# Attention, Fourier mixing and feed-forward: scores made once, probabilities and normalized rows turned by transfers

## The chip, the cores and the metric

The kernel runs on one core of a Trainium2 chip. The metric is the device time of one execution in microseconds (us). TensorE (PE) multiplies matrices into PSUM, eight banks of 128 partitions by 2 KB; VectorE (DVE), ScalarE (ACT) and GpSimd (POOL) work on tiles of up to 128 partitions in SBUF; transfers run on 16 DMA engines and are issued from the queues of SyncE (SP), ACT and POOL. Each queue takes its instructions in order, so an instruction that waits holds up what stands behind it.

## The reference

Inputs are q, k and v of 8 batches, 8 heads, 576 positions, 64 values a head, and two weight matrices of 512 x 2048 and 2048 x 512, all float32.

1. Attention by heads, with a mask by blocks of 64 positions: position i sees j where `i // 64 >= j // 64`. Scores are scaled by 1/8, the maximum of a row is subtracted, then come the exponential, the division by the row's sum (plus 1e-9) and the product with v.
2. The heads are put side by side: x has 8 x 576 x 512.
3. `u = x + real(fft(fft(x, axis=1), axis=2))`.
4. `un = (u - mean) / sqrt(var + 1e-6)` along the 512 values.
5. `out = u + max(un @ w_ch1, 0) @ w_ch2`.

## The kernel before

**Precision.** float32 operands are cut in two parts that are multiplied apart: a rounded part and a rest, or a high and a low half in f16. So a score is `LEAD x LEAD` plus one matmul of 128 rows in which `REST` holds rest and rounded part stacked, and an f16 product is three matmuls (high x high, high x low, low x high).

**A head.** `load_head` (line 288) brings q and k, turned on the host, to `raw` (64 x 1152). `lead` rounds it on ACT into one of three `LEAD` buffers, two transfers copy its halves into `REST` (`lead_copies`), and DVE and POOL write the rests (`rest`). Rows 64 to 71 of `LEAD` hold constants that put the mask into the product. Then comes a first pass for the maxima, `max_part`: matmuls of `LEAD` alone, with queries on the partitions, six of them with 1600 columns in all, and reductions on DVE into `M`. `shift` turns `M` (128 x 5) by a matmul with the identity, scales it on ACT and sends it by a transfer into row 72 of `LEAD`. In the second pass `scores` makes the scores again, now in both parts and with keys on the partitions, since the values need keys there; row 72 subtracts the maximum within the product. ACT takes the exponential twice, to f16 (`ph`) and to float32, and POOL subtracts them (`pl`). `values` multiplies with v in 15 pairs of blocks, three matmuls each, into one bank `av`; DVE divides by the sum, and for each second head two transfers store the pair to a buffer `xd` in DRAM.

**A batch.** When its eight heads are stored, `mirror` loads the rows and, by POOL's indirect transfers, their mirror images; sums and differences go through cosine and sine matrices (`stage1`, `stage2_sin`, `stage2_cos`). `normalized_steps` takes two row tiles of 128 at a time, normalizes them (`norm`), and `turn` turns each with four matmuls with the identity into a bank, from which ACT takes the high half `uh` and DVE the low half `ul`. There are 18 such pairs, 36 tiles. Each pair gives a stretch of feed-forward work (`feed_steps`): 192 matmuls of 256 columns (into bank `h`) and 96 of 512 (into bank `acc`).

**Weights.** In the front 18 loads of the weights (14 of 1 MB, 4 of 512 KB) are issued from SP, three in flight, and DVE, ACT and POOL cut them in two parts.

**Order.** A planner in the kernel writes the order of PE's instructions. Each `Step` has a cost on PE, a chain of what follows on other engines (`D`, `A`, `G`, `Q` for DVE, ACT, POOL and SP's queue with a time, `L` for a transfer's landing, `B` for the point where its bank is free) and the steps that it must follow. Lanes (loads, preparing, maxima, scores, values, transforms) hand over their next step; the planner takes the one that is ready by its own clock, and fills with feed-forward matmuls when none is. On the chip PE takes matmuls in this order, whatever the other engines are late by. Before all weights have landed no second batch's heads are begun. Banks: three named `ps`, two `h`, two `acc`; from the first feed-forward step on only `ps` serve attention and transforms.

Of the kernel before, what the change touches and what calls it, by code (L numbers as in the profile page):

```python
# [44 lines left out]
KM = D + 8  # L45
KS = KM + 1

# [24 lines left out]
def _constants():  # L72
# [45 lines left out]
    masks = np.zeros((9, 64 + 2 * S))  # L118
    masks[8, 64 + S:] = 1.0
    for c in range(4):  # L120
        masks[c, 64 + 128 * c:128 + 128 * c] = 1.0
        masks[c, 64 + S + 128 * c + 64:64 + S + 128 * c + 128] = NEG
        masks[4 + c, 128 + 128 * c:192 + 128 * c] = 1.0
        masks[4 + c, 64 + S + 128 * c + 128:64 + S + 128 * c + 192] = NEG
# [6 lines left out]
        "c_id": np.eye(P, dtype=np.float32),  # L131
# [5 lines left out]
class Step:  # L137
# [8 lines left out]
    bank: bool = False  # L146
# [32 lines left out]
def tile_attn_fourier_ffn(  # L179
    ctx: ExitStack, tc: tile.TileContext, qk, v, w1, w2, c_dft, c_masks, c_id, c_rows, out  # L180
# [9 lines left out]
    def ps_tile():  # L190
        return ps[current].tile([P, 512], F32, name=current)
# [4 lines left out]
    def tp(*args, **kw):  # L196
        return tc.keep_in_program_order(nc.tensor.transpose(*args, **kw))  # L197


    ident = const.tile([P, P], F32, name="ident")  # L200
    nc.sync.dma_start(ident, c_id)
# [21 lines left out]
    NB = 3  # L223
    LEAD = [const.tile([KS, 64 + 2 * S], F32R, name=f"lead{i}") for i in range(NB)]
    REST = [const.tile([P, 2 * S], F32R, name=f"rest{i}") for i in range(NB)]
    M = [const.tile([P, 6], F32, name=f"M_{i}") for i in range(2)]
# [4 lines left out]
    for i in range(NB):  # L231
        nc.gpsimd.dma_start(LEAD[i][D:KS], c_masks)
        nc.vector.tensor_scalar(LEAD[i][0:D, 0:64], ones[0:D, 0:64], 0.0, None, op0=ALU.mult)
    for i in range(2):
        nc.vector.memset(VH[i][:, 0:4, :, D:D + 1], 1.0)
        nc.vector.memset(VH[i][0:64, 4, :, D:D + 1], 0.0)
        nc.vector.memset(VH[i][64:128, 4, :, D:D + 1], 1.0)
# [12 lines left out]
    current = "ps"  # L250
# [5 lines left out]

    def ready(step):
        r = max((done[x] for x in step.after), default=0.0)
        return max(r, min(rings[x][0] for x in lent)) if step.bank else r

    def issue(step):
# [15 lines left out]
        if step.bank:  # L277
            current = min(lent, key=lambda x: rings[x][0])
            rings[current] = rings[current][1:] + [t if free is None else free]
# [15 lines left out]
    def quick(h):  # L295

        return nc.scalar if h < H else nc.sync

    def lead_copies(h):
        x0, x1 = REST[h % NB].bitcast(F32), LEAD[h % NB].bitcast(F32)  # L300
        quick(h).dma_start(x0[D:P, 0:S], x1[0:D, 64:64 + S])
        quick(h).dma_start(x0[0:D, S:], x1[0:D, 64 + S:])

    def rest(h, which):

        x0, x1, raw = REST[h % NB], LEAD[h % NB].bitcast(F32), raws[h]
        if which == 0:
            nc.vector.tensor_tensor(x0[0:D, 0:S], raw[:, 0:S], x1[0:D, 64:64 + S], op=ALU.subtract)  # L308
        else:
            nc.gpsimd.tensor_tensor(x0[D:P, S:], raw[:, S:], x1[0:D, 64 + S:], op=ALU.subtract)  # L310
# [38 lines left out]
    def prepare_lane():  # L349
        for h in range(B * H):  # L350
            yield Step(
                lambda: lead(h), 0.0, ("A1.15",), (("L", h),), ("T", h), place=h - 1.0,
                need=(("S", h - NB, 2),) if h >= NB else (),
            )
            yield Step(lambda: lead_copies(h), 0.0, ("A1.0" if h < H else "Q1.2", "L2.2"), (("T", h),), ("TC", h), place=h - 0.9)
# [3 lines left out]
    def v_lane():  # L359
        for g in range(B * H // 2):  # L360
# [4 lines left out]
                       need=(("V", 2 * g - 3, 4),) if g > 1 else ())  # L365
            yield Step(
                lambda: split_v(g), 0.11, ("D0.46", "B", "A0.83", "D0.88"), (("NS", g),), ("N", g), True,
                need=(("V", 2 * g - 3, 4),) if g > 1 else (), place=2 * g - 0.4,
            )

    def max_part(h, n):

        m = M[h % 2]
        x = LEAD[h % NB][0:KM]
        kh = x[:, 64 + S:]
        qh = lambda j: x[:, P * j:P * (j + 1)]
        t = ps_tile()

        parts = MAXPARTS[n]
        at = 0  # L380
        for i, (j, lo, hi) in enumerate(parts):
            mm(
                t[:, at:at + hi - lo], qh(j), kh[:, lo:hi], start=(i == 0), stop=(i == len(parts) - 1),
                skip_group_check=True,
            )
            at += hi - lo
        if n == 0:
            nc.vector.tensor_reduce(
                m[:, 0:6:5], t[:, 0:128].rearrange("p (x y) -> p x y", y=64), axis=AX.X, op=ALU.max
            )  # L390
        j, lo, hi = parts[-1]
        nc.vector.tensor_reduce(m[:, j:j + 1], t[:, at - hi:at], axis=AX.X, op=ALU.max)  # L392
        if n == 3:
            nc.vector.tensor_tensor(m[:, 4:5], m[:, 4:5], m[:, 5:6], op=ALU.max)

    MAXPARTS = (((0, 0, 64), (4, 512, 576), (1, 0, 192)), ((2, 0, 320),), ((3, 0, 448),), ((4, 0, 512),))

    def shift(h):

        t = ps_tile()  # L400
        tp(t[0:5, 0:P], M[h % 2][:, 0:5], ident)
        mt = work.tile([5, P], F32R, name="mt", bufs=2)
        nc.scalar.activation(mt, t[0:5, 0:P], AF.Copy, bias=float(8.0 * PSHIFT * np.log(2.0)), scale=-1.0)
        dst = LEAD[h % NB][KM:KS, 0:640].rearrange("r (j p) -> r j p", j=5)
        quick(h).dma_start(dst.bitcast(F32), mt.bitcast(F32))

    probs = {}

    CHUNKS = (0, 1, 4, 2, 3)
    PIECES = (
        (0, 0, ((0, 0, 288),)), (0, 288, ((0, 288, 288),)),
        (1, 0, ((1, 0, 448), (4, 0, 64))), (2, 0, ((2, 0, 320), (3, 0, 192))),
    )

    def scores(h, n):

        x0, x1 = REST[h % NB], LEAD[h % NB]
        i, at, chunks = PIECES[n]  # L420
        if at == 0:
            width = S if i == 0 else 512
            probs[h, i] = [work.tile([P, width], F16, name=f"p{x}{i}", bufs=1) for x in "hl"]
        ph, pl = probs[h, i]
        t = ps_tile()
        w = 0
        for c, lo, width in chunks:
            first, last = P * c + lo, P * c + lo + width
            keys = S + (P * c if c < 4 else S - P)
            mm(t[:, w:w + width], x0[:, keys:keys + P], x0[:, first:last], start=(w == 0), stop=False, skip_group_check=True)  # L430
            keys, w = keys + 64, w + width
            mm(t[:, w - width:w], x1[:, keys:keys + P], x1[:, 64 + first:64 + last], start=False, stop=True, skip_group_check=True)
        p32 = work.tile([P, 512], F32, name="p32", bufs=2)
        nc.scalar.activation(ph[:, at:at + w], t[:, 0:w], AF.Exp, scale=0.125)  # L434
        nc.scalar.activation(p32[:, 0:w], t[:, 0:w], AF.Exp, scale=0.125)  # L435
        nc.gpsimd.tensor_tensor(pl[:, at:at + w], p32[:, 0:w], ph[:, at:at + w], op=ALU.subtract)  # L436
# [4 lines left out]
    def values(h, at):  # L441
# [6 lines left out]
        c = CHUNKS[at]  # L448
# [12 lines left out]
        if at < 4:  # L461
            return
# [215 lines left out]
    def normalized_steps(us, keys, stores, place):  # L678
# [17 lines left out]
        def turn(i):  # L696
            un = uns.pop(i)
            if i == 0:
                parts.extend(work.tile([P, NK, 2, P], F16, name=x, bufs=2) for x in ("uh", "ul"))
# [313 lines left out]
```

## Time and profile before

Times and profile are of the program on the chip; a share of busy time is of the span.

| | us |
|---|---|
| median of three runs | 1312.41 (1312.14 to 1313.05) |
| profiled execution | 1315.5 |
| its span | 1313.7 |
| PE busy | 1184.2 (90%) |
| DVE busy | 671.9 (51%) |
| ACT busy | 548.5 (42%) |
| POOL busy | 530.0 (40%) |
| DMA: moved bytes | 99.10 MB, 75 GB/s on average |

In the rows of the profile, L194 is the helper that issues every matmul and L197 the one that issues every turn on PE, so matmuls are told apart by their tiles: `ps<-lead 72*128` is the first pass, `73*128` with `rest` the second, `ident,M` the turn of the maxima, `ident,un` that of normalized rows. SPq stands for SP's queue. A group shows its busy time in us, the mean of one in ns, then the idle time of the engine ahead of it and what ended that. The start of a row in a timeline is counted from the start of the span.

### The profile page before, as it was taken

The page shows a single profiled execution, that of the slowest core. Times are in us where ns is not written, and L with a number is a line of the kernel's source. Part 1 is how long each engine was busy: PE and PEld are TensorE (multiplying, and loading weights), DVE is VectorE, ACT ScalarE, POOL GpSimd, SP SyncE. Part 2 cuts the span into 40 slices and gives each one's busy share as a digit, 9 for nine tenths or more (in the row PEclk, how much of TensorE's full clock was granted, in tenths as well). Part 3 has the DMA queues.
Part 4 walks back from the last instruction along what each step waited for, and adds up shares of the span by engine and source line. Part 5 has one row for each costly group of instructions (what it writes and reads, how often), then busy time and mean ns, then how long its engine had stood idle before and what let it go on. Part 6 is the DMA issues. An engine that isn't in the chain of part 4 may idle for free.

```text
span 1313.7 us, 25264 instructions
## 1 busy us (share of the span) xinstructions
PE 1184.2 (90%) x10068; PEld 886.7 (67%) x10068; DVE 671.9 (51%) x1440; ACT 548.5 (42%) x1137; POOL 530.0 (40%) x578
## 2 busy tenths in 40 slices
PE   3464469999898999999999999999899999999998
PEld 2363357777676777677777777777677767767665
DVE  6983776445645564655546544746372432412211
ACT  3569355545354444444545354544543112111110
POOL 4668143444544553455443645436442500300000
PEclk9955679999699999999999999999999999999999
DMA  9756213232223223322242133223211000000000
GB/s 280 230 175 177 93 29 77 84 106 64 61 65 92 76 50 90 93 76 51 80 115 75 44 96 104 73 70 86 79 30 49 30 12 17 22 1 17 16 17 17
DMA packets 55941, 99.10 MB, mean 75 GB/s; under 512 B 7709, under 2 KB 26605, under 8 KB 55696
## 3 DMA queue, kind: packets, MB, share of 16 engines
q1 hardware_dynamic: 52176, 87.56, 23.5%
q0 software_dynamic: 2288, 7.54, 1.9%
q10 hardware_dynamic: 1360, 2.38, 0.6%
q8 instruction: 80, 1.31, 0.4%
q14 instruction: 37, 0.30, 0.1%
HBM read 58.46 MB, written 18.87 MB: 59 GB/s over the span
## 4 chain that ended last, share of the span: by engine, by line
PE 76%; DVE 10%; ACT 4%; DMA 3%; POOL 3%; issue 3%; SPq 0%; ACTq 0%; DVEq 0%; POOLq 0%
PE h L194 27%; PE acc L194 26%; PE ps L194 16%; PE av L194 5%; POOL pl L436 2%; PE ps L197 1%; DVE M L392 1%; DVE W L837 1%; DMA W<-in_moe_w_ch_dram 1%; DVE rest L308 1%; DVE W L838 1%; ACT lead L293 1%; DVE tmp L549 1%; DMA U<-xd,rows 1%; DVE W L836 1%
## 5 line engine op out<-in xcount | busy, mean ns | idle before, releaser
L194 PE MATMUL h<-uh,W 128*128 128x256 f16 x2304 | 434.9, 275 | 0.0
L436 POOL TENSOR_TENSOR pl<-p,ph 128x288 f16<-128x288 f32 (+1 forms) x256 | 257.9, 1017 | 395.8 <-ACT p L435 249.6
L194 PEld LDWEIGHTS <-W 128*128 128x128 f16 x3456 | 325.8, 99 | 64.3 <-issue 4.0
L194 PE MATMUL acc<-W,gh 128*128 128x512 f16 x1152 | 347.2, 383 | 0.0
L194 PE MATMUL h<-ul,W 128*128 128x256 f16 x1152 | 316.2, 274 | 0.0
L194 PE MATMUL acc<-W,gl 128*128 128x512 f16 x576 | 220.1, 382 | 0.4 <-DVE gl L750 0.4
L750 DVE SCALAR_TENSOR_TENSOR gl<-h,gh 128x512 f16<-128x512 f32 x144 | 98.9, 687 | 227.3 <-ACT gh L749 227.2
L194 PE MATMUL ps<-lead 72*128 72x64 f32 (+9 forms) x700 | 196.5, 342 | 12.5 <-ACT lead L293 6.8
L749 ACT ACTIVATE gh<-h 128x512 f16<-128x512 f32 x144 | 85.9, 596 | 268.4 <-PE h L194 267.7
L434 ACT ACTIVATE ph<-ps 128x512 f16<-128x512 f32 (+1 forms) x229 | 116.0, 507 | 121.0 <-PE ps L194 119.7
L194 PEld LDWEIGHTS <-gh 128*128 128x128 f16 x1152 | 101.0, 99 | 87.8 <-issue 8.2
L392 DVE TENSOR_REDUCE M<-ps 128x1 f32<-128x320 f32 (+3 forms) x235 | 120.5, 527 | 47.9 <-PE ps L194 46.7
L194 PE MATMUL av<-VH,pl 128*128 128x65 f16 x960 | 115.9, 200 | 31.7 <-POOL pl L436 31.5
L194 PEld LDWEIGHTS ps<-lead 72*128 72x128 f32 (+1 forms) x700 | 125.6, 201 | 20.8 <-ACT lead L293 6.8
L194 PEld LDWEIGHTS <-ph 128*128 128x128 f16 x1920 | 113.0, 103 | 34.1 <-DVE x L474 8.4
L310 POOL TENSOR_TENSOR rest<-raw,lead 64x576 fp32r<-64x576 f32 x64 | 116.2, 1816 | 23.3 <-ACT lead L293 18.5
L194 PE MATMUL av<-VH,ph 128*128 128x65 f16 x960 | 118.1, 202 | 8.2 <-DVE x L474 7.6
L194 PE MATMUL ps<-rest 128*128 128x64 f32 (+2 forms) x345 | 121.6, 360 | 1.8 <-DVE M L392 1.1
L435 ACT ACTIVATE p<-ps 128x512 f32<-128x512 f32 (+1 forms) x229 | 115.9, 506 | 10.2 <-POOL pl L436 10.1
L194 PE MATMUL av<-VL,ph 128*128 128x64 f16 x960 | 117.3, 200 | 0.0
L194 PEld LDWEIGHTS <-pl 128*128 128x128 f16 x960 | 93.6, 102 | 34.9 <-POOL pl L436 34.8
L308 DVE TENSOR_TENSOR rest<-raw,lead 64x576 fp32r<-64x576 f32 x64 | 60.0, 938 | 88.4 <-ACT lead L293 88.3
(171 smaller groups left out, 1376.7 us busy)
## 6 DMA issues: line engine op xcount, KB each, us to landing
raw<-in_qk_dram SPq DMA_DIRECT2D x64, 288.0 KB
rest<-lead SPq DMA_DIRECT2D x112, 144.0 KB
W<-in_moe_w_ch_dram SPq DMA_DIRECT2D x14, 1024.0 KB
V<-in_v_dram SPq DMA_DIRECT2D x32, 320.0 KB
xd<-x SPq DMA_DIRECT2D x32, 256.0 KB
out_dram<-u SPq DMA_DIRECT2D x32, 256.0 KB
u<-xd SPq DMA_DIRECT2D x8, 512.0 KB
dft<-in_c_dft_dram POOLq DMA_DIRECT2D x1, 2606.0 KB, 11.3
```

Of the source, the lines that this page charges most:

```text
L194: return tc.keep_in_program_order(nc.tensor.matmul(*args, **kw))
L197: return tc.keep_in_program_order(nc.tensor.transpose(*args, **kw))
L293: nc.scalar.copy(LEAD[h % NB][0:D, 64:], raws[h])
L308: nc.vector.tensor_tensor(x0[0:D, 0:S], raw[:, 0:S], x1[0:D, 64:64 + S], op=ALU.subtract)
L310: nc.gpsimd.tensor_tensor(x0[D:P, S:], raw[:, S:], x1[0:D, 64 + S:], op=ALU.subtract)
L392: nc.vector.tensor_reduce(m[:, j:j + 1], t[:, at - hi:at], axis=AX.X, op=ALU.max)
L434: nc.scalar.activation(ph[:, at:at + w], t[:, 0:w], AF.Exp, scale=0.125)
L435: nc.scalar.activation(p32[:, 0:w], t[:, 0:w], AF.Exp, scale=0.125)
L436: nc.gpsimd.tensor_tensor(pl[:, at:at + w], p32[:, 0:w], ph[:, at:at + w], op=ALU.subtract)
L549: nc.vector.tensor_tensor(e[0:r], X[c][0:r], U[c][0:r], op=op)
L749: nc.scalar.activation(gh, t, AF.Relu)
L750: nc.vector.scalar_tensor_tensor(gl, t, 0.0, gh, op0=ALU.max, op1=ALU.subtract)
```

## The change

The scores are made once, in both parts, with queries on the partitions. The maxima are taken from them; the exponential takes `-max/8 + 5 ln 2` as a bias, one value a partition. High and low half of the probabilities are written, query by query, into a tile `PROB` (two sets of three tiles: query blocks 4, 0 and 1 in 1024 columns, block 3 in 512, block 2 in 384). One transfer per tile, issued from SP's queue, turns both halves, piece of 128 x 128 by piece, into `TURN` (one set), and `values` reads `TURN`. The key blocks are shifted by 64 rows so that the half block stands first; columns that the mask hides are set to zero once. The first pass, the turn of the maxima and its transfer are gone; `LEAD` has 68 rows, and there are two `LEAD` and `REST` in place of three. The copies of the first eight heads go from ACT's queue to SP's, the weight loads from SP's to ACT's. Of the normalized rows, ACT and DVE now make both halves before the turn, and one transfer from SP's queue turns the two; the identity matrix is gone. The space for POOL's DMA descriptors goes from 8192 to 2048.

```diff
-KM = D + 8
-KS = KM + 1
+KM = D + 4
+SCORES = (
+    (((4, 0, 288), (1, 0, 192)), ((4, 288, 576), (0, 0, 64))),
+    (((3, 0, 448),),),
+    (((2, 0, 320),),),
+)
+WIDTHS = (1024, 512, 384)
+BLOCKS = (((4, 0), (0, 640), (1, 768)), ((3, 0),), ((2, 0),))
...
-    NB = 3
+    NB = 2
+    PROB = [[const.tile([P, 2, w], F16, name=f"prob{i}_{x}") for i, w in enumerate(WIDTHS)] for x in range(2)]
+    TURN = [const.tile([P, 2 * w // P, P], F16, name=f"turn{i}") for i, w in enumerate(WIDTHS)]
...
     def lead_copies(h):
-        quick(h).dma_start(x0[D:P, 0:S], x1[0:D, 64:64 + S])
-        quick(h).dma_start(x0[0:D, S:], x1[0:D, 64 + S:])
+        nc.sync.dma_start(x0[D:P, 64:64 + S], x1[0:D, 64:64 + S])
+        nc.sync.dma_start(x0[0:D, 64 + S:], x1[0:D, 64 + S:])
...
-    def max_part(h, n):
...
-    def shift(h):
...
     def scores(h, n):
         x0, x1 = REST[h % NB], LEAD[h % NB]
+        prob = PROB[h % 2][n]
+        m = work.tile([P, 8], F32, name="M", bufs=2)
+        places = []
+        for parts in SCORES[n]:
+            t = ps_tile()
+            at = 0
+            for i, (j, lo, hi) in enumerate(parts):
+                q, k = slice(P * j, P * (j + 1)), slice(64 + S + lo, 64 + S + hi)
+                to = t[:, at:at + hi - lo]
+                mm(to, x0[:, q], x0[:, k], start=(i == 0), stop=False, skip_group_check=True)
+                mm(to, x1[:, q], x1[:, k], start=False, stop=(i == len(parts) - 1), skip_group_check=True)
+                places.append((j, lo, hi, to))
+                at += hi - lo
+        chunks = [j for j, at in BLOCKS[n]]
+        for j, lo, hi, x in places:
+            i = 3 if lo else chunks.index(j)
+            nc.vector.tensor_reduce(m[:, i:i + 1], x, axis=AX.X, op=ALU.max)
...
+        nc.vector.tensor_scalar(
+            bias, m[:, 0:len(chunks)], -0.125, float(PSHIFT * np.log(2.0)), op0=ALU.mult, op1=ALU.add
+        )
+        for c, (j, at) in enumerate(BLOCKS[n]):
+            for j_, lo, hi, x in places:
+                if j_ == j:
+                    p32 = work.tile([P, 448], F32, name="p32", bufs=2)[:, 0:hi - lo]
+                    ph, pl = (prob[:, i, at + 64 + lo:at + 64 + hi] for i in range(2))
+                    for to in (ph, p32):
+                        nc.scalar.activation(to, x, AF.Exp, bias=bias[:, c:c + 1], scale=0.125)
+                    nc.gpsimd.tensor_tensor(pl, p32, ph, op=ALU.subtract)
+
+    def turn(h, n):
+        nc.sync.dma_start_transpose(TURN[n], PROB[h % 2][n].rearrange("p x w -> p (x w)"))
...
     def score_lane():
+                    ((f"D{(2.0, 0.85, 0.72)[n]}", f"A{(2.9, 1.15, 0.92)[n]}", "B", f"G{(0.6, 1.08, 0.85)[n]}")),
+                    (("TC", h), ("T2", h, 0), ("T2", h, 1)) + ((("S", h - 2, n),) if h > 1 else ()), ("E", h, n), len(SCORES[n]),
...
+    def turn_lane():
+                    lambda n=n: turn(h, n), 0.0, (f"Q{(1.5, 0.8, 0.6)[n]}", "L2.5"), (("E", h, n),), ("S", h, n),
+                    need=(("V", h - 1, n),) if h else (), place=h,
...
-        def turn(i):
+        def split(i):
             un = uns.pop(i)
-            uh, ul = parts
-            t = ps_tile()
-            for c in range(NK):
-                tp(t[:, P * c:P * (c + 1)], un[:, P * c:P * (c + 1)], ident)
-            tv = t.rearrange("p (c n) -> p c n", c=NK)
-            nc.scalar.copy(uh[:, :, i], tv)
-            nc.vector.tensor_tensor(ul[:, :, i], tv, uh[:, :, i], op=ALU.subtract)
+            hl = work.tile([P, DM], F32, name="tmp", bufs=2).bitcast(F16).rearrange("p (x n) -> p x n", x=2)
+            nc.scalar.copy(hl[:, 0], un)
+            nc.vector.tensor_tensor(hl[:, 1], un, hl[:, 0], op=ALU.subtract)
+            nc.sync.dma_start_transpose(
+                parts[0][:, :, :, i].rearrange("p x c n -> p (x c) n"), hl.rearrange("p x n -> p (x n)")
+            )
...
-                lambda i=i: turn(i), 0.45, ("A0.6", "D0.7"), (("n", me, i),), ("t", me, i), True,
+                lambda i=i: split(i), 0.0, ("A0.6", "D0.7", "Q0.5", "L2.2"), (("n", me, i),), ("t", me, i),
...
     def weight_loads(done):
-            nc.sync.dma_start(raw(x).rearrange("p (j n) -> p j n", j=n), weight(i, n))
+            nc.scalar.dma_start(raw(x).rearrange("p (j n) -> p j n", j=n), weight(i, n))
...
-    nc = _bacc.Bacc("TRN2", target_bir_lowering=False, num_devices=1, dynamic_dma_scratch_size=8192)
+    nc = _bacc.Bacc("TRN2", target_bir_lowering=False, num_devices=1, dynamic_dma_scratch_size=2048)
```

197 lines of the change are left out of this document (74 added, 123 removed).

## The prediction

> **What bounds the kernel now.** I read the page first, then the busy time by stage, then the waits of TensorE, and last single stretches of its queue.
>
> ```profile
> span 1313.7 us, 25264 instructions
> PE 1184.2 (90%) x10068; PEld 886.7 (67%) x10068; DVE 671.9 (51%) x1440; ACT 548.5 (42%) x1137; POOL 530.0 (40%) x578
> PE   3464469999898999999999999999899999999998
> PEclk9955679999699999999999999999999999999999
> ```
>
> PE is the busiest engine by far, but its first six slices (some 200 us) are at three to six tenths, and the granted clock falls to 0.5 there. So the program has a front that something else sets, and a rest that PE sets. I cut it at 180 us, where the first feed-forward matmuls begin, and at 1000 us, where the last attention matmuls end:
>
> ```profile
> 0.00:180.00 180.00, 87.06 (x688) 73.91 (x688) 131.10 (x258) 100.16 (x200) 102.72 (x103) 0.75 0.58 177
> 180.00:1000.00 820.00, 787.90 (x7206) 598.98 (x7206) 456.49 (x1029) 400.83 (x847) 395.55 (x423) 0.98 0.28 75
> 1000.00:1313.70 313.70, 309.21 (x2179) 213.79 (x2176) 84.33 (x154) 47.46 (x91) 31.76 (x53) 1.00 0.06 18
> ```
>
> The columns are PE, PEld, DVE, ACT, POOL, clock, DMA share, GB/s. In the middle stage PE lacks 32 us of 820; in the last one it runs feed-forward matmuls that wait for nothing. In the middle, DVE is at 56%, ACT at 49%, POOL at 48%, DMA at 28%: none of them is near its end. In the front DVE has 131 of 180 us, DMA 58%.
>
> **What is taken from PE.** Removed are the matmuls of the first pass, which served the row maximum alone (6 a head, 1600 columns), one turn of the maxima a head, and four turns a row tile of the normalized rows. Matmuls overlap, so busy times (450 ns for one of 448 columns) overstate them; I take the distance from the start of one to the start of what follows, in an undisturbed stretch:
>
> ```profile
> 607.59 0.27 PE L197 MATMUL ps<-ident,M 128*5 128x128 f32 x1
> 607.62 0.56 PE L194 MATMUL ps<-lead 72*128 72x64 f32 x3
> 608.02 0.28 PE L194 MATMUL h<-uh,W 128*128 128x256 f16 x1
> ...
> 621.78 0.39 PE L194 MATMUL ps<-lead 72*128 72x320 f32 x1
> 622.02 0.28 PE L194 MATMUL h<-uh,W 128*128 128x256 f16 x1
> ...
> 622.61 0.45 PE L194 MATMUL ps<-lead 72*128 72x448 f32 x1
> 622.90 0.20 PE L194 MATMUL av<-VH,ph 128*128 128x65 f16 x1
> ...
> 623.36 0.47 PE L194 MATMUL ps<-lead 72*128 72x512 f32 x1
> 623.68 0.28 PE L194 MATMUL h<-uh,W 128*128 128x256 f16 x1
> ...
> 631.73 0.63 PE L197 MATMUL ps<-ident,un 128*128 128x128 f32 x4
> 632.20 0.27 PE L194 MATMUL h<-uh,W 128*128 128x256 f16 x1
> ```
>
> The turn of the maxima with the three small matmuls costs 608.02 - 607.59 = 0.43 us, then 0.24, 0.29 and 0.32: 1.28 us a head. The first 8 heads lie in the front, where PE has time to spare; 56 heads give 72 us. Four turns of a normalized tile cost 0.47 us; 36 tiles give 17 us, all behind 172 us. Together **89 us** less on PE where PE is the bound. What stays is equal: the scores are still 1600 columns in 6 pairs of matmuls, the values still 15 triples of 64 or 65 columns.
>
> **What the other engines get.** The maxima are now taken from the full scores, and the exponentials take them as a bias, so they are cut by query blocks: 6 pieces (288, 288, 192, 64, 448, 320) in place of 4 (288, 288, 512, 512).
>
> ```profile
> L392 DVE TENSOR_REDUCE M<-ps 128x1 f32<-128x448 f32 x59 | 36.5, 618 | 9.3 <-PE ps L194 8.1
> L392 DVE TENSOR_REDUCE M<-ps 128x1 f32<-128x320 f32 x61 | 29.6, 485 | 22.4 <-PE ps L194 22.4
> L471 DVE TENSOR_SCALAR DEN<-av,vacc 128x5 f32<-128x5 f32 x64 | 14.0, 219 | 30.6 <-PE av L194 30.5
> L434 ACT ACTIVATE ph<-ps 128x512 f16<-128x512 f32 x116 | 69.7, 601 | 42.8 <-PE ps L194 41.7
> L434 ACT ACTIVATE ph<-ps 128x288 f16<-128x288 f32 x113 | 46.3, 410 | 78.2 <-PE ps L194 77.9
> L436 POOL TENSOR_TENSOR pl<-p,ph 128x512 f16<-128x512 f32 x128 | 154.8, 1217 | 66.1 <-ACT p L435 54.4 <-PE ps L194 9.6
> L436 POOL TENSOR_TENSOR pl<-p,ph 128x288 f16<-128x288 f32 x128 | 103.4, 818 | 329.7 <-ACT p L435 195.1 <-issue 122.5 <-PE ps L194 7.4
> ```
>
> DVE's two rows of reductions give 1.04 ns a column and 0.15 us at no width. It reduces the same 1600 columns in one piece more, and has three small scalings more, at the price of the small row below them: 0.15 + 3 x 0.219 = 0.8 us a head. On ACT the two rows give a slope of 0.85 ns a column and 0.17 us at no width; two pieces more, each exponentiated twice, add 4 x 0.17 = 0.66 us, less a small copy of the turned maxima. On POOL the intercept is 0.31 us, so 0.6 us a head. For 56 heads that is 45, 25 and 35 us on engines that have 360 to 425 us free in the middle stage. PE's own work hides them, at nothing; with that cover gone, DVE's 0.8 us lies within a head's chain. A head's first scores now hold two banks of PSUM and not one from the matmuls through reductions and exponentials, some 5 us; feed-forward matmuls have their own banks and fill PE meanwhile, so I take nothing for that.
>
> **What the turns cost.** Each head gets three transfers that turn probabilities: 16, 8 and 6 pieces of 128 x 128 in two parts, 128 x 3840 f16 or 983 KB; each normalized tile gets one of 262 KB. All stand in SP's queue. The trace has no turning transfer. The nearest is this pair of plain ones, 288 KB together in runs of 512 bytes, and the load that waits for them:
>
> ```profile
> 406.04 0.38 SPq L479 DMA_DIRECT2D xd<-x  x1
> 406.48 0.50 SPq L482 DMA_DIRECT2D xd<-x  x1
> 408.37 0.38 SPq L535 DMA_DIRECT2D u<-xd  x1
> ```
>
> and one microsecond of it by the busy time in a window (the last two columns are the share of the 16 DMA engines and GB/s):
>
> ```profile
> 407.00:408.00 1.00, 1.00 (x10) 0.88 (x10) 0.00 (x0) 1.00 (x4) 0.37 (x1) 1.00 0.91 276
> ```
>
> They land 2.33 us after the first issue, and at a 0.91 share move 276 GB/s, so 303 GB/s at full share. Lower bound: one issue of 0.4 us and that rate. The large turn (524 KB) then takes 2.33 + 236/303 = 3.1 us, a head moves its 983 KB in 3.2 us, 63 MB in all; beside 28% DMA in the stage that is far from full (a head has 820/56 = 14.6 us). Upper bound: every piece of 128 x 128 costs an issue of its own, 30 x 0.38 = 11.4 us a head. The order of PE's queue is written by a planner in the kernel that allows the large turn 1.5 us of queue and 2.5 us to land, so 4.0. At the lower bound the values find their operands 0.9 us early; PE, which takes its matmuls in the written order, waits only if a turn is late.
>
> [...]
>
> What makes it late is its queue. SP's waits in the middle stage:
>
> ```profile
> SPq L301 <- PE ps L194: 148.8, 41, 10.4
> SPq L314 <- DVE VL L340: 85.7, 19, 12.9
> SPq L479 <- DVE x L474: 57.7, 17, 6.1
> ```
>
> SP stands at the copies of the next head's rounded inputs, at the loads of V and at the stores of a pair of heads, 3.4 to 4.5 us each time. Before, the row of shifts stood in the same queue; now the turns do, and behind them the next head's copies and loads, and behind those its scores. A turned tile exists once, so a turn also waits until PE has done the values of the head before. I let one head in three meet such a wait ahead of its turn, 3.6 us on average, 0.9 us of it covered: 19 x 2.7 = **51 us of new PE waits**. That one in three is my choice, between none (PE lacks 32 us in the stage today) and every head (56 x 2.7 = 151 us).
>
> **The front.** Eight heads are done before the first transform. They lose a hop each, the row of shifts, which PE waited for:
>
> ```profile
> PE ps L197 <- DVE M L394: 14.8, 3, 9.7
> PE h L194 <- DMA lead<-mt: 9.8, 1, 9.8
> ```
>
> That bounds the gain at 25 us. On the other side, DVE gets 8 x 0.8 = 6 us, and the weight loads move from SP's queue to ACT's, where their issues stand before exponentials:
>
> ```profile
> 45.06 8.20 SPq L826 DMA_DIRECT2D W<-in_moe_w_ch_dram  x3
> 129.84 9.13 SPq L826 DMA_DIRECT2D u<-in_moe_w_ch_dram  x4
> ```
>
> Seven of the 18 issues took 17 us of a queue, since three loads of 1 MB are in flight; ACT is busy 100 of 180 us, so much is covered, and ACT loses the 24 small issues of the first heads, about 14 us. Eight heads' turns are 7.9 MB, 26 us at 303 GB/s, onto 104 us of DMA time. Bounds -25 to +20 us; I take the middle and a little for a head's new last hop, **+5**. Two input buffers in place of three I take at nothing: the scores of a head, the last readers, are made before the second next head is copied, a head's length later. The smaller ring for POOL's descriptors I take at nothing too, POOL being idle for 77 of the 180 us.
>
> **Sum.** Profiled execution 1315.5 us, 1.8 around its span. 1315.5 - 89 + 51 + 5 = 1282.5; it stands 3.1 above the median of the runs, so **1279 us**.
>
> **Rivals.** (a) *Every turn is late; slower.* Place: PE's queue at each head's first values. Price: an issue by pieces, half the upper bound, 0.19 us a piece. The large turn then holds SP 3.0 us and lands at about 4.9, and SP's work a head rises from some 2 us (four and a half plain issues of 0.4 to 0.5 us: two copies, a load, half a load of V, half of two stores) to 2 + 30 x 0.19 = 7.7 us, with the tiles' 36 x 8 pieces over 64 heads 8.6 us, so waits pile up; 2.5 us late a head, my estimate from 4.9 against 4.0 and one more wait in two heads, makes 56 x 2.5 = 140 us: 1312 - 89 + 5 + 140 = 1368 us. It decides against the change from 84/56 = 1.5 us a head. For it: the long SP waits above. Against it: 0.4 us for an issue of any size in every plain row. (b) *SP is the bound.* At the full 0.38 us a piece a head needs 2 + 11.4 + 1.7 = 15.1 us of SP, against the (820 - 89)/56 = 13.1 us in which PE would be through with it. The middle stage then is 846 us and not 731: 1312 - 89 + 5 + 115 = 1343 us if no wait comes on top, 1494 us with the 151 us from above; I take the middle, 1420 us. (c) *Pieces run one after another.* 30 pieces a head at the 1.9 us from the second issue above to its landing is 57 us a head, 64 heads 3650 us; against it stands that plain transfers overlap. [...] (d) *The chain of a head, not PE, sets the pace*, so what PE loses is idle: no gain, about 1312. Against it: PE is 96% busy in the middle and feed-forward work for 313 us is left when attention ends.
>
> [...]
>
> **How the numbers follow.** Forecast 0.52, own range 1222 to 1309 (waits of 0 to 81 us with the front at +5, or a front off by some 20 with waits near my choice); (a) 0.28; (b) 0.13; (c) 0.02; (d), or a give-back that just eats the 89 us, 0.05. Faster by over 0.2% 0.52, within 0.2% (2.6 us, about what can be told from no change) 0.05, slower 0.43. The range reaches from 1222, no waits at all, to 1400, most of (a), and leaves out most of (b) and (c).
>
> **What would show it.** Right: PE's busy time down by some 130 to 150 us in the groups of 72 rows and of the identity, with PE still over 90% in the middle, turns issued in about 0.5 us and landing in 3 to 4. Wrong: PE's waits at the values, for the turned tile, over 84 us; turns that hold SP for microseconds (a), SP without idle time (b), a DMA share near full (c), a first feed-forward matmul well behind 200 us (front).

## The result, and the profile after

The changed kernel takes 1348.11 us in the median (1345.13 to 1350.36) against 1312.73 us: a ratio of 1.0267, 95% interval 1.0253 to 1.0281. It is slower; 1279 us was forecast, and rival (a) stood at 1368. Here and below a median is of all executions of a kernel, while a ratio leaves out those more than 1.5% above its fastest, which matters only for e14 and e16, whose ten executions spread over 36 and 33 us.

The page of the changed kernel: span, busy times, the share of the DMA engines over the span and the count of packets.

```profile
span 1346.2 us, 25020 instructions
PE 1125.7 (84%) x9476; PEld 819.4 (61%) x9476; DVE 709.0 (53%) x1697; ACT 622.8 (46%) x1329; POOL 565.7 (42%) x715
DMA  9999446985498769747989848886542011101100
DMA packets 345048, 171.13 MB, mean 127 GB/s; under 512 B 297280, under 2 KB 315728, under 8 KB 344800
```

PE's busy time fell by 58 us, not by 130 to 150. (That mark had added up rows that overlap; by the prediction's own distances some 99 us could go, the 89 and 10 of the first eight heads.) The DMA engines, 28% busy in the middle stage before, are at four to nine tenths in the slices after the front while attention runs, 75% in the mean, and of all packets 86% have under 512 bytes. By stage, with the columns of the prediction (behind the length of the stage the busy times of PE, PEld, DVE, ACT and POOL, then clock, DMA share and GB/s):

```profile
0.00:180.00 180.00, 66.85 (x540) 56.83 (x540) 122.18 (x261) 98.96 (x203) 89.87 (x117) 0.99 0.81 213
180.00:1000.00 820.00, 719.67 (x6604) 531.22 (x6605) 489.58 (x1259) 468.73 (x1022) 443.43 (x545) 0.92 0.75 150
1000.00:1346.20 346.20, 339.14 (x2335) 231.31 (x2332) 97.24 (x177) 55.07 (x105) 32.39 (x54) 1.00 0.12 27
```

Attention's last matmul begins at 998.5 us; before, the last values came at 1007. What was lost shows in the last stage: 339.1 us of PE's work is left there and not 309.2. So in the first 1000 us PE did at least 30 us less of feed-forward work, though attention asked less of it. In the middle stage PE lacks 100 us of 820 and not 32, and its granted clock is 0.92 and not 0.98. PE's longest waits in that stage (total, times, longest):

```profile
PE av L201 <- DMA turn<-prob: 48.7, 27, 5.3
PE ps L201 <- ACT p L419: 39.0, 24, 4.6
PE h L201 <- DMA un_t<-tmp: 11.5, 1, 11.5
```

The values wait for turned tiles, the next scores for exponentials that still read their bank. The same wait stands in the front too, from 0 to 180 us:

```profile
PE av L201 <- DMA turn<-prob: 44.1, 11, 9.1
```

How long the issues take shows in the timeline of SP's queue (begin, us):

```profile
544.92 3.06 SPq L424 DMA_TRANSPOSE turn<-prob  x1
...
548.71 1.31 SPq L424 DMA_TRANSPOSE turn<-prob  x1
...
551.71 1.21 SPq L424 DMA_TRANSPOSE turn<-prob  x1
```

And the list of DMA issues, whose last number is the median from issue to landing:

```profile
turn<-prob SPq DMA_TRANSPOSE x192, 4.2
```

The large turn of a head holds SP's queue for 3.1 us, the smaller ones for 1.2 to 1.3; the plain issues between 500 and 600 us took 0.4 to 0.7, but for one of 1.1. In the last stage, where nothing else moves, the turns of two normalized tiles (524 KB together) stand alone:

```profile
1253.82 2.62 SPq L690 DMA_TRANSPOSE un_t<-tmp  x2
```

The same place in steps of 1 us:

```profile
1254.82:1255.82 1.00, 1.00 (x7) 0.47 (x5) 0.28 (x1) 0.00 (x0) 0.00 (x0) 1.00 0.88 165
1255.82:1256.82 1.00, 1.00 (x7) 0.41 (x5) 0.00 (x0) 0.00 (x0) 0.00 (x0) 1.00 0.98 183
1256.82:1257.82 1.00, 1.00 (x6) 0.49 (x5) 0.00 (x0) 0.00 (x0) 0.00 (x0) 1.00 0.95 177
```

The DMA share is the last number but one. The three shares add up to 2.8 us of all engines, so 187 GB/s, or 22 ns of one engine for each of 2048 packets of 256 bytes. By that rate a head's 983 KB need 5.3 us of all engines, an estimate.

### The profile page after: what moved, and what is told of

The parts are those of the page before. It is cut to its first block, busy times and chain, and to the rows that moved or that the text cites. A ratio compares the mean times of both kernels' runs of the same rounds, so it can differ in the third digit from the quotient of the medians.

```text
span 1346.2 us, 25020 instructions
## 1 busy us (share of the span) xinstructions
PE 1125.7 (84%) x9476; PEld 819.4 (61%) x9476; DVE 709.0 (53%) x1697; ACT 622.8 (46%) x1329; POOL 565.7 (42%) x715
## 2 busy tenths in 40 slices
DMA packets 345048, 171.13 MB, mean 127 GB/s; under 512 B 297280, under 2 KB 315728, under 8 KB 344800
## 4 chain that ended last, share of the span: by engine, by line
PE 55%; DMA 16%; DVE 14%; issue 5%; ACT 5%; POOL 4%; SPq 2%; DVEq 0%; ACTq 0%; POOLq 0%
PE acc L201 22%; PE h L201 21%; PE ps L201 8%; DMA turn<-prob 8%; PE av L201 4%; DVE M L405 2%; DMA u<-xd,rows 2%; DMA un_t<-tmp 2%; POOL prob L420 1%; DMA W<-in_moe_w_ch_dram 1%; ACT p L419 1%; DVE tmp L535 1%; DMA rest<-lead 1%; ACT prob L419 1%; DVE rest L322 1%
## 5 line engine op out<-in xcount | busy, mean ns | idle before, releaser
L201 PE MATMUL h<-un_t,W 128*128 128x256 f16 x3456 | 425.6, 276 | 11.5 <-DMA un_t<-tmp 11.5
L420 POOL TENSOR_TENSOR prob<-p,prob 128x288 f16<-128x288 f32 (+4 forms) x384 | 295.6, 777 | 253.4 <-ACT p L419 236.4
L419 ACT ACTIVATE prob<-ps,M 128x64 f16<-128x64 f32 (+2 forms) x358 | 164.5, 492 | 151.5 <-DVE M L410 147.3
L201 PE MATMUL av<-VH,turn 128*128 128x65 f16 x1920 | 136.5, 209 | 105.9 <-DMA turn<-prob 92.8
L201 PEld LDWEIGHTS <-turn 128*128 128x128 f16 x2880 | 122.7, 108 | 138.8 <-DMA turn<-prob 109.8
L405 DVE TENSOR_REDUCE M<-ps 128x1 f32<-128x288 f32 (+2 forms) x358 | 138.8, 425 | 86.1 <-PE ps L201 70.2
L419 ACT ACTIVATE p<-ps,M 128x64 f32<-128x64 f32 (+2 forms) x358 | 171.0, 491 | 24.6 <-POOL prob L420 22.7
L201 PE MATMUL ps<-rest 128*128 128x288 f32 (+2 forms) x358 | 126.5, 369 | 42.7 <-ACT p L419 34.8
L201 PE MATMUL av<-VL,turn 128*128 128x64 f16 x960 | 124.1, 208 | 0.0
L201 PE MATMUL ps<-lead 68*128 68x288 f32 (+2 forms) x358 | 105.5, 329 | 0.0
```

What stands on the lines that cost most here:

```text
L201: return tc.keep_in_program_order(nc.tensor.matmul(*args, **kw))
L405: nc.vector.tensor_reduce(m[:, i:i + 1], x, axis=AX.X, op=ALU.max)
L419: nc.scalar.activation(to, x, AF.Exp, bias=bias[:, c:c + 1], scale=0.125)
L420: nc.gpsimd.tensor_tensor(pl, p32, ph, op=ALU.subtract)
```

## The experiments

Theory T: the turned tiles land late, since their small packets fill the DMA engines. Theory O: PE's written order expects them too early. Theory B: a head's chain behind the scores (reductions, exponentials, the banks held meanwhile) became longer. "Retimed" means that the planner was given the times that the profile shows in place of its own; that writes a new order for PE. "Plain copies" carry the same bytes to the same places and leave out the turning; they show time alone. Ratios are to the kernel before, runs of the same chip, with 95% intervals.

| run | what differs | us | ratio |
|---|---|---|---|
| changed kernel | | 1348.1 | 1.0267 (1.0253 to 1.0281) |
| e4_rows_only | before, with rows by transfers | 1298.6 | 0.9876 (0.9854 to 0.9898) |
| e5_attention_only | changed, with rows on PE | 1318.0 | 1.0036 (1.0016 to 1.0056) |
| e10_attention_retimed | e5, turns retimed | 1344.3 | 1.0225 (1.0200 to 1.0251) |
| e1_plain_rows | changed, plain copies in long rows | 1305.6 | 0.9931 (0.9910 to 0.9951) |
| e2_plain_256 | changed, plain copies in 256 bytes | 1326.3 | 1.0114 (1.0072 to 1.0156) |
| e15_half_retimed | changed, turns half retimed | 1332.2 | 1.0132 (1.0109 to 1.0155) |
| e3_retimed_turns | changed, turns retimed | 1324.5 | 1.0080 (1.0049 to 1.0112) |
| e3b_retimed_all | e3, exponentials retimed too | 1319.1 | 1.0041 (1.0028 to 1.0053) |
| e6_bank_order | e3, exponentials bank by bank | 1324.3 | 1.0090 (1.0056 to 1.0125) |
| e8_plain_retimed | e3b with plain copies | 1308.4 | 0.9957 (0.9942 to 0.9972) |
| e12_one_exp | e8, one exponential | 1263.2 | 0.9624 (0.9603 to 0.9645) |
| e13_no_max | e8, no maxima | 1257.3 | 0.9553 (0.9525 to 0.9582) |
| e14_no_max_turned | changed, no maxima | 1330.2 | 1.0057 (1.0019 to 1.0095) |
| e16_no_max_turned_retimed | e3b, no maxima | 1303.8 | 0.9840 (0.9801 to 0.9879) |
| e9_four_banks | e3b, 4 banks and 1 | 1433.8 | 1.0915 (1.0894 to 1.0936) |
| e9c_rows_four_banks | e4, 4 banks and 1 | 1358.2 | 1.0346 (1.0324 to 1.0367) |

### The transfers: e1 and e2

```diff
-        nc.sync.dma_start_transpose(TURN[n], PROB[h % 2][n].rearrange("p x w -> p (x w)"))
+        nc.sync.dma_start(TURN[n].rearrange("p b n -> p (b n)"), PROB[h % 2][n].rearrange("p x w -> p (x w)"))
```

> The changed kernel with the three transfers of probabilities a head made plain copies of the same tiles in the same places (rows of 1.5 to 4 KB a partition), so its probabilities are not turned; all else stays, PE's order too. Theory T (turned tiles land late, since their 283 thousand packets of 256 bytes fill the DMA engines): DMA share in 180 to 1000 us falls from 0.75 to about 0.35, a transfer lands in about 3 us in place of 4.2, PE's waits for the turned tile (48.7 us in the middle stage, 44 in the front) fall under 15, the granted clock goes back to 0.97, time 1265 to 1290. Rival B (a head's chain through reductions, exponentials and PSUM banks): waits move to the banks, time 1325 or more.

e2 keeps the pieces of 128 columns apart in the destination:

```diff
+    TURN = [const.tile([P, 2 * w // P, P + 8], ...)[:, :, 0:P] for ...]
+        nc.sync.dma_start(TURN[n], PROB[h % 2][n].rearrange("p x w -> p (x w)").rearrange("p (b n) -> p b n", n=P))
```

> As the first run, plain copies that do not turn, but cut into runs of 256 bytes by a gap of 16 bytes between the pieces of the destination: the same number of packets as the turning transfers. If the size of the packets is the price: DMA share 0.7 to 0.8 in the middle, landing about 4 us, time 1335 to 1350, like the changed kernel. If turning itself is the price: like the run with long rows, 1265 to 1290.

Long rows gave back 42 us, less than the 58 to 83 expected, and the waits and the share stayed above what was expected too. e1 in the middle stage, its DMA share last but one, and then PE's two longest waits in it:

```profile
180.00:1000.00 820.00, 749.39 (x6870) 552.15 (x6871) 502.74 (x1282) 471.68 (x1031) 437.05 (x542) 0.94 0.53 152
```

```profile
PE ps L201 <- ACT p L419: 34.3, 24, 5.1
PE av L201 <- DMA turn<-prob: 24.8, 18, 3.5
```

The waits for turned tiles halve, the share falls from 0.75 to 0.53 with the same bytes, and the waits for exponentials stay. e2, with the same bytes in nearly as many packets as the turns (341,976 in the run, against 345,048), lies in the middle, at a share of 0.63 and 4.4 us to landing: neither expectation held. Of the 42 us some 21 go with the size of the packets and some 22 with the turning itself. But PE's waits in e2's middle stage are not in the middle:

```profile
PE av L201 <- DMA turn<-prob: 55.8, 35, 4.4
PE ps L201 <- ACT p L419: 26.4, 21, 6.3
```

Its waits for turned tiles are longer than the changed kernel's, and those for exponentials shorter, so one wait's size does not tell the time. All three kernels have the same order of PE. T holds for part of the loss.

### The order: e3, e15, e3b, e6

The old line stands on the left, the new one on the right, both cut to the part that differs:

```diff
-  f"Q{(1.5, 0.8, 0.6)[n]}", "L2.5"          +  f"Q{(3.1, 1.3, 1.25)[n]}", "L3.0"
-  ("A0.6", "D0.7", "Q0.5", "L2.2")          +  ("A0.6", "D0.8", "Q1.3", "L3.1")
```

> The changed kernel, complete, with the planner told what the profile shows of the turns: 3.1, 1.3 and 1.25 us of queue and 3.0 us to land (in place of 1.5, 0.8, 0.6 and 2.5), rows 1.3 and 3.1. Theory O (PE's order is written for turns that land too early): PE's waits for turned tiles fall from 48.7 to under 20 us in the middle stage, filled with feed-forward matmuls, time 1290 to 1315. Theory T with a full DMA as the bound: waits stay over 40, time 1340 or more. Rival B (banks): turn waits fall, waits for exponentials (37 us) stay or grow, time 1320 to 1340.

> The changed kernel, complete, with half of the retiming of the turns (2.3, 1.05, 0.95 us of queue, 2.75 to land; rows 0.9 and 2.65). If lateness against the order counts in proportion: between 1324 and 1348, some 1336. If each order is a draw of its own, with a scatter of 20 us: anywhere from 1315 to 1355.

Telling the planner the measured times gave 24 us, half of the step 16. PE's waits in the middle stage of e3:

```profile
PE ps L201 <- ACT p L419: 45.7, 35, 4.2
PE av L201 <- DMA turn<-prob: 16.0, 11, 2.7
```

The waits for turned tiles fall as O expects, from 49 to 16 us, and those for exponentials grow from 39 to 46. How much of the 24 us is owed to that is less sure, since a new order can also lose as much (e10 below). e3b adds the exponentials' and subtractions' times:

```diff
-  f"A{(2.9, 1.15, 0.92)[n]}"  f"G{(0.6, 1.08, 0.85)[n]}"      +  f"A{(4.2, 1.45, 1.2)[n]}"  f"G{(0.65, 1.15, 1.05)[n]}"
```

> The changed kernel, complete, with the turns' times as in the retimed run and the exponentials' and subtractions' too (ACT 4.2, 1.45, 1.2 us a piece in place of 2.9, 1.15, 0.92; POOL 0.65, 1.15, 1.05). Theory: the planner frees a bank of PSUM too early, so PE stands at the next scores until the exponentials are done (46 us in the middle stage of the retimed run). Then these waits fall under 20 us and the time to 1295 to 1312. Rival: the banks are short whatever the plan says; waits stay over 35, or PE lacks feed-forward work to fill with, time 1318 to 1330.

It gave 5 us more, and the waits for exponentials were 51.6 us, so they are not a slip of the plan that such numbers mend. (These are the times of the work itself; a plan that also allows for the waits in DVE's and ACT's queues was not tried.) e6 takes e3's exponentials bank by bank:

```diff
-        for c, (j, at) in enumerate(BLOCKS[n]):
-            for j_, lo, hi, x in places:
+        for j_, lo, hi, x in places:
+            for c, (j, at) in enumerate(BLOCKS[n]):
```

> The run with retimed turns, its exponentials taken bank by bank (blocks 4, 1, then 4, 0) and not block by block, so that the first of the two banks comes free two pieces earlier; nothing else is changed. Theory banks: PE's waits for exponentials fall from 46 to about 30 us and the time by 10 to 20, to 1305 to 1315. Rival: it is the exponentials' late start (reductions on DVE) that counts, not the order: 1320 to 1328, the same waits.

Nothing moved, as the rival expected: 46.9 us of waits, 1324.3 us.

### The parts apart: e4, e5, e10

e4 is the kernel before with `split` in place of `turn` for the rows and the retimed costs for it; e5 the changed kernel with the rows' old `turn`; e10 is e5 with the retimed turns.

> The kernel before with one part of the change alone: the normalized rows split first and turned by one transfer a tile. 36 x 0.47 us less on PE: if the transfer lies behind feed-forward work, 1312 - 17 = 1295 to 1300. Rival: each pair's feed-forward start waits for the transfer in PE's order, or the lower clock eats it: 1308 to 1318.

> The changed kernel with the normalized rows turned on PE as before: scores made once and probabilities turned by transfers alone. If the parts add up (rows alone gave 1298.6 against 1313, so 14 to 16 us): 1360 to 1366. If both share the queue and the DMA engines, so that the tiles' transfers make the probabilities later: 1340 to 1350.

> The run with attention alone (1318.0) with the turns retimed (3.1, 1.3, 1.25 us of queue, 3.0 to land). If the early order of the values is the loss in it too: PE's waits for turned tiles fall from 38 to under 15 us in the middle stage, time 1298 to 1308. If what is left is banks and clock: 1312 to 1320.

The rows alone are worth 16 us, as the sum had them. Attention alone costs 5 us (ratio 1.0036), and both together 35: the parts do not add, and neither expectation for e5 held. With the rows' transfers in, PE's waits for turned tiles in the middle rise from 38 to 49 us and those for exponentials from 24 to 39. And e10 went the wrong way: retiming cut the waits for turned tiles from 38 to 17 us, as expected, but those for exponentials rose from 24 to 45, and the kernel was 26 us slower. So a new order alone can move some 20 us from one wait to the other and change the time by some 25 us either way. Why this one lost as much as e3 gained isn't settled, and the differences between kernels of different orders (e3, e3b, e15, and e4 and e5 against the whole) are uncertain by about as much. e1, e2, e6, e12, e13, e14 and e16 each keep the order of the kernel that they start from; the cause rests on them.

### The chain behind the scores: e8, e12, e13, e14, e16

> Plain copies in long rows in place of the turns of probabilities (which are then not turned), together with all planner times of the retimed run. What is left above the ideal is then neither packets nor early orders. If those two are all that was missed: 1240 to 1275. If the chain of a head (reductions, exponentials, banks) and the lower clock are a loss of their own: 1285 to 1305.

e8 has both remedies, plain copies and all times, and yet takes 1308 us. PE's two longest waits in the middle stage are no longer for transfers:

```profile
PE ps L201 <- ACT p L419: 53.5, 19, 7.3
PE h L201 <- ACT tmp L337: 13.6, 1, 13.6
```

From here one engine's share was taken out of the chain with the order left as it was. e12 leaves out the second exponential (and with it some 20 us of POOL's time), e13 the maxima. This is e12's edit; e13 drops the reductions and takes a constant as the bias:

```diff
-                    for to in (ph, p32):
-                        nc.scalar.activation(to, x, AF.Exp, bias=bias[:, c:c + 1], scale=0.125)
-                    nc.gpsimd.tensor_tensor(pl, p32, ph, op=ALU.subtract)
+                    nc.scalar.activation(ph, x, AF.Exp, bias=bias[:, c:c + 1], scale=0.125)
+                    nc.gpsimd.tensor_tensor(pl, ph, ph, op=ALU.subtract)
```

> The run with plain copies and all times retimed (1308.4), with the second exponential left out: POOL subtracts the f16 probabilities from themselves, so the low halves are zero; six exponentials a head in place of twelve, PE's order the same. Theory chain (ACT's exponentials hold the banks): PE's waits for exponentials fall from 53 to under 25 us, time 1270 to 1285. Rival (the exponentials start late because DVE's reductions are late): waits over 40, time 1298 to 1308.

> The run with plain copies and all times retimed (1308.4), with the row maxima left out: a constant bias, no reductions, so exponentials follow the scores at once; PE's order the same. Theory that DVE's place in the chain is what was added: waits for exponentials fall from 53 to under 20 us, time 1260 to 1285. Rival (ACT and the order): waits over 40, time 1298 to 1308.

Both gave more than expected, 45 and 51 us. The middle stage and then PE's waits for exponentials, first of e12, then of e13:

```profile
180.00:1000.00 820.00, 772.23 (x7174) 577.75 (x7175) 516.07 (x1311) 351.33 (x706) 426.30 (x559) 0.96 0.54 152
```

```profile
PE ps L201 <- ACT prob L417: 19.1, 14, 4.7
```

```profile
180.00:1000.00 820.00, 773.01 (x7156) 576.91 (x7155) 390.52 (x750) 468.76 (x1029) 448.44 (x557) 0.96 0.52 151
```

```profile
PE ps L201 <- ACT p L411: 23.5, 16, 3.7
```

Waits for exponentials fall from 54 to 19 and 24 us, and the granted clock rises from 0.93 to 0.96. Relief on either engine, with the same plan, does about the same. Then the transfers came back in:

> The changed kernel with its own plan and its turning transfers, the row maxima left out alone (a constant bias). If the chain behind the scores is the second half of the loss: turns start some 2 us earlier than PE's order allows for, waits for turned tiles fall from 49 to under 20 and for exponentials from 39 to under 20, time 1270 to 1295. If the full DMA engines set the pace: 1330 or more.

> The changed kernel with its turning transfers and all planner times retimed (1319.1), the row maxima left out (a constant bias). If the chain is the larger limit and turns cost only by coming late: about 10 us above the run with plain copies and no maxima, 1262 to 1275. If packets of 256 bytes in a nearly full DMA are a limit of their own, hidden behind the chain so far: 1285 to 1315.

Leaving out the maxima from the changed kernel itself gave 18 us by the medians and some 28 by the ratios (1.0267 to 1.0057); the waits for exponentials fell to 16.5 us as expected, but 40.7 us of waits for turned tiles were left. With the retimed order the four corners are, by the medians:

| | maxima | no maxima |
|---|---|---|
| turned | 1319 | 1304 |
| plain copies | 1308 | 1257 |

Taking the turns away gives 11 us with the long chain and 47 with the short one; taking the maxima away gives 15 with the turns and 51 without. (By the ratios e16 stands at 1292 us, and the four differences are 11, 38, 26 and 53.) Each of the two limits hides much of the other.

Part of that lies in the front. The rows from 0 to 180 us, of e13 and then of e16:

```profile
0.00:180.00 180.00, 69.21 (x578) 61.05 (x579) 116.02 (x200) 113.43 (x232) 112.83 (x131) 0.82 0.74 227
```

```profile
0.00:180.00 180.00, 58.10 (x488) 50.97 (x488) 93.20 (x149) 96.54 (x196) 93.91 (x110) 1.00 0.97 213
```

With the short chain and the turns the DMA engines are full in the front, where the weights are loaded too, and the first feed-forward matmul begins at 208.7 us, in e13 at 177.2. PE is idle 32 us longer in e16 than in e13, and 23 of them lie before 220 us. So this corner shows the turns beside the weight loads at least as much as a limit of the middle stage.

### Banks: e9 and e9c

```diff
-BANKS = {"ps": 3, "h": 2, "acc": 2}
+BANKS = {"ps": 4, "h": 1, "acc": 2}
-                    after = ... + ((("g", me, f - 4),) if f > 3 else ())
+                    after = ... + ((("g", me, f - 2),) if f > 1 else ())
```

> The changed kernel, complete, with all planner times retimed, and one PSUM bank more for scores and transforms (four), taken from the feed-forward's first stage, which then has one in place of two; the plan knows it. Theory banks (two of three banks are held by a head's first scores through reductions and exponentials): PE's waits for exponentials fall from 52 us to under 20, time from 1319 to 1280 to 1300. Rival: the waits are for ACT's exponentials of the same head's tiles whatever the banks, or one bank for the first stage costs as much: 1312 to 1335.

> The control for it: the run with the rows alone (1298.6) with the same four and one banks. What it shows is the price of one bank for the first stage where banks are no bound (waits for exponentials 3 us there): 1298 to 1303 if the first stage's evacuation hides behind the second stage's matmuls, 1320 or more if PE waits at each pair of first stages.

The control alone lost 60 us, the changed kernel 115: one bank for the first stage of the feed-forward is dear (or its order is), so this does not tell what a fourth bank is worth by itself. What it does show: PE's waits for exponentials were 55.9 us with four banks, as with three. That a missing bank is what PE waits for stays open; that a shorter chain helps is what e12 and e13 show.

## Why the prediction was wrong

**Less work on PE, 89 us: the size holds where it could be seen.** The rows' 17 us came out as 17.1 us less PE time and 16 us in all (e4). With plain copies and no maxima, e13 stands at 1257 us, 56 below the kernel before, so a large part of the 89 us is there to be had. But it is work that PE no longer does, not time.

**The cost of the turns: the first step that failed.** The prediction took the rate of the nearest transfer, 303 GB/s, and asked how many bytes; the same row says that 512 bytes took 27 ns of an engine (0.91 us x 16 engines for 276 KB, 539 packets). Turned packets have some 256 bytes (72.03 MB more than before in 345,048 less 55,941 packets, 249 bytes in the mean) and take 22 ns alone and 25 in the whole run: the shares of the queues, 59.5% of 1346.2 us and 26.5% of 1313.7 us, differ by 453 us of 16 engines, or 25 ns a packet. So the rate is 160 to 190 GB/s, a head takes 5.3 us of all engines and not 3.2, and the large turn holds SP for 3.1 us and not 0.4. With it "far from full" fell: the share is 0.75 and above 0.9 in whole slices. The small packets that a turn is made of should have been counted, not its bytes: e1, without them and without turning, is 42 us faster.

**The waits for turns, 51 us: near in the middle stage by luck, and not the whole.** They came to 48.7 us there, and to 44.1 in the front, where the sum had next to nothing for them; together 93 us, above the 84 that the prediction named as a sign of being wrong. The reason given, waits in SP's queue ahead of a turn in one head of three, was only a part: e3, with the same queue and an order that allows for 3.1 us of issue, brings them to 16 us, e1, with shorter transfers, to 25.

**The chain, taken at nothing: the second step that failed.** "PE's own work hides them" was said of the new reductions, scalings and exponentials, and "I take nothing" of the two banks held for 5 us. The exponentials' group in the changed kernel, and then one head by its timeline:

```profile
L419 ACT ACTIVATE prob<-ps,M 128x288 f16<-128x288 f32 x119 | 59.6, 501 | 76.4 <-DVE M L410 72.9 <-DMA out_dram<-u 2.2 <-DMA xd<-x 1.0
```

```profile
545.74 0.38 PE L201 MATMUL ps<-rest 128*128 128x288 f32 x1
...
552.22 1.20 DVE L405 TENSOR_REDUCE M<-ps 128x1 f32<-128x288 f32 x4
...
557.62 0.51 ACT L419 ACTIVATE p<-ps,M 128x288 f32<-128x288 f32 x1
```

The exponential with a bias from a tile takes 501 ns at 288 columns where it took 410 without one; with that and two pieces more a head, ACT got 74 us more and not 25. The prediction left those 91 ns out. Worse is the waiting between: here the scores begin at 545.74, DVE reduces at 552.22, behind other work in its queue, and the second half of block 4 is exponentiated until 558.13; the small pieces in the same two banks follow until 560.86. The banks are held for 13 to 15 us, not 5. In this head PE went on with values and feed-forward matmuls from 551.58; where its written order has the next scores at such a place, it stands, which makes the 39 us of waits for exponentials. The cover named (PE's work) was there on average and not at those places. What a shorter chain is worth, e12 and e13 measured: 45 and 51 us with plain copies; e14, with the turns, 18 to 28.

**The clock, not in the sum: the third.** An example from the same place; behind the length of the window stands PE's busy time, and the granted clock is the last number but two:

```profile
542.00:546.00 4.00, 4.00 (x30) 2.74 (x29) 2.78 (x4) 2.89 (x5) 2.12 (x4) 1.00 0.73 158
546.50:551.50 5.00, 1.35 (x6) 0.86 (x6) 4.90 (x12) 1.32 (x3) 3.58 (x4) 0.92 1.11 174
551.50:555.50 4.00, 3.92 (x44) 3.17 (x45) 3.72 (x11) 1.60 (x3) 0.18 (x1) 0.50 0.91 169
```

After 5 us in which PE was busy for 1.35, the clock is granted at 0.50 for 4 us. Matmuls show it: the 24 of a head's first values begin between 537.28 and 537.97, 0.69 us, ahead of such a gap, and between 551.58 and 552.80, 1.22 us, behind this one. Over the middle stage, busy time times what the clock lacks, in steps of 4 us, is 45 us after and 15 before, in 16 stretches below 0.9 and 5. Most stretches last 4 to 15 us; the longest, 199 to 240 us at 0.50, holds 12 of the 45 us. So a wait was paid for nearly one and a half times: 68 us more of idle time went with 30 us of slower matmuls. In the front the row's 0.99 can't be taken as it stands: there, too, 24 values begin over 1.24 us (111.76 to 113.00), the slow pace.

**The front, +5 us: right by its own mark alone.** The first feed-forward matmul begins at 185.0 us and not 180.5. But PE is idle 20 us more before 180 us (some 10 of them are the first eight heads' first pass, which is gone), and 22 us more from there to 260 us (26.4 and not 4.2 of 80).

**The sum again.** PE's idle time grew by 20 us in the front, 68 in the middle stage and 3 in the last, 91 in all; its busy time fell by 58.5; that is the 32.5 us between the spans. The sum had 51 us of waits and 5 in the front against 89 us less work. Of the busy time, 89 and 10 us (the first eight heads) are work that is gone and 30 came back by the clock of the middle stage; some 10 us were not placed, and may be the clock of the front. The low end of the prediction's range does not follow from its own terms: no waits at all make 1279 - 51 = 1228 us and not 1222. That does not bear on the miss.

**The rivals.** (a) was the nearest, in size and in place; its price of an issue, 0.19 us a piece, came close (3.1 us for 16 pieces, 1.3 for 8 and 1.2 for 6, against 3.0, 1.5 and 1.1). But its 140 us of waits at the values were 49 in the middle stage, and lateness is not the whole: removing it gave 24 to 42 us of the 124 that separate 1348 from 1313 less the 89. (b) did not come: SP stood in waits for other engines for some 450 of the 820 us of the middle stage, 188 of them for POOL's subtraction. (c) is refuted: a row tile's eight pieces land in 4.4 us in the median, where one after another would take 15. (d), a head's chain as the pace, was given almost no chance as the end of the gain; it is the second limit, which e12 and e13 show.

## What to carry to other kernels

Price a transfer by its packets at the ns that a packet of the nearest size takes in the trace (here 27 ns at 512 bytes, 22 to 25 at 256), and put the time of issue beside it (here 1.2 to 3.1 us for a turn of probabilities). Less work on the engine that binds need not be less time: here PE was busy for 58 us less, and the kernel took 35 us more. So ask how much longer each result's chain to its next reader becomes, and what stands in the queue at that place. There may be one limit behind the other, as the four corners show. Here the part without a chain (the normalized rows alone) gave 1.2%, and was faster than both kernels; the part that put a turn and a longer chain between a matmul and its reader gave its gain back.

## What was not expected of the hardware

A plain copy of the same bytes in runs of 256 bytes (e2) left the DMA engines at a share of 0.63 in the middle stage, where the turning transfers had 0.75 and long rows (e1) 0.53. An exponential whose bias comes from a tile took 91 ns more, at 288 columns, than one without (501 and 410). And a gap in PE's work (1.35 us busy of 5) was followed by 4 us at a granted clock of 0.50; over the middle stage 68 us of added waits went with 30 us of slower matmuls. A row's clock can also mislead: at 0.99 in the front, 24 values begin over 1.24 us, as over 1.22 at a granted clock of 0.50 and not over 0.69 as at 1.00.
